# The first chunk's up product as plain 512-column products: a change at the start of a fused attention and mixture-of-experts kernel

## Chip, cores, metric

One core of a Trainium2 chip. The metric is device microseconds of one execution. The kernel before takes 1763.5 us in the runs beside the changed kernel. Repeats of one kernel differ by 1 to 3 us, so differences below about 2 us need several runs and some care.

## The reference

An attention without softmax feeds a mixture of four experts (float32 throughout):

```python
kv  = einsum('bhsd,bhse->bhde', k, v)        # (8, 8, 64, 64); q, k, v: (8, 8, 576, 64)
o   = einsum('bhsd,bhde->bhse', q, kv)
o   = o / sqrt(mean(o*o, -1) + 1e-6) * g_norm
x   = o.transpose(0, 2, 1, 3).reshape(4608, 512)
p   = domain_probs / (domain_probs.sum(-1) + 1e-9)
for e in range(4):                           # w1: (4, 512, 1024), w2: (4, 1024, 512)
    out += p[:, e:e+1] * (relu(x @ w1[e]) @ w2[e])
```

## The kernel before

The 4608 rows of x are cut into nine chunks of 512. A *stage* is one chunk with one expert, and there are 36 of them. Each stage has an **up product** (x by w1), a ReLU and a **down product** (by w2). Attention for the next chunk is mixed into the stages of expert 0.

The up product saves multiplications with Strassen's scheme, used twice: seven times seven products in place of eight times eight. Each of the 49 is done as two matmuls of 128x128x128, 98 in all. For this it needs sums of blocks of w1 and sums of blocks of x, and its results have to be totalled again by VectorE and ScalarE:

```python
for i, m in enumerate(OUTER):                 # 7 outer products
    for j, mm in enumerate(ORDER):            # 7 inner products
        def product(eng, ...):
            for u in range(2):
                nc.tensor.matmul(ps.ap[:, u*P:(u+1)*P],            # 128 columns
                    lhsT=w1f[e][m][mm][1]()[:, u*P:(u+1)*P], rhs=views[m][mm][1](), ...)
        # ... cut: copies out of PSUM (ScalarE), totals (VectorE)
```

Nothing is issued in program order. Each operation is given to a planner with a **key**, its wished place in units of stages. `plan.layout` sorts each engine's work by key, places it by modelled durations, and picks the buffers. An operation may be given to "either" VectorE or GpSimd; that choice, too, is the planner's. While the next operation's key is below 0 and TensorE has nothing to do, the planner puts in **dummies**, two transposes of the identity into an idle bank:

```python
attention(0, -2.0, 1.3, 0.1)                  # chunk 0's attention
weights_1(0, -2.5, 0.02, -0.35)               # loads of w1[0], and sums of its blocks (key -0.35)
x_views = {0: x_forms(0, -0.3)}               # sums of blocks of chunk 0's x
...                                           # cut: for each stage s: attention(c + 1), up, down
order = plan.layout(slots, later, idle, ("u1", "u2", "db"), 0.0)   # dummies' banks; up to key 0
```

PSUM has eight banks in four pairs: u1 and u2 (up), db (down), ab (attention and down).

## Time and profile before

| | before |
|---|---|
| median of the runs beside the changed kernel | 1763.53 us (1762.25 to 1764.72, 4 runs) |
| span of the profiled run | 1762.9 us |
| TensorE lost, 0 to 130 us | 36.0 us |
| TensorE lost after 130 us | some 5 us at the very end, the same after the change |

"Lost" needs a word, since the busy share hides it. The profile counts a dummy as busy, and counts a matmul at half clock as busy too. I therefore count the passes of every shape in a stretch (a float32 product is recorded as two passes; a pass that crosses the end of a stretch is shared out between the two) and multiply by the pace of that shape at full clock (us per pass: 512 columns 0.430, 256 0.2163, 128 0.1117, the attention's 96x64 0.0355, 64x64 0.098). That is the *work*; the stretch less the work, dummies not counted as work, is the *loss*. Four stretches are used: up to 25.6 us (loads pace chunk 0's attention), 25.6 to 62.6, 62.6 to 92, and 92 to 130 us.

### The profile page before, as it was taken

How to read it: one execution, taken by the hardware profiler on the slowest of the kernel's cores; microseconds unless marked ns; L12 is line 12 of the kernel's file. 1: busy time of each engine (PE TensorE's matmuls, PEld its weight loads, DVE VectorE, ACT ScalarE, POOL GpSimd, SP SyncE). 2: the span in 40 equal slices, each digit the busy share in tenths (PEclk: the TensorE clock that was granted, in tenths of full speed). 3: DMA queues.
4: the chain of work that ended last, by engine and by line, in shares of the span. 5: the costliest groups of instructions: out<-in, count | busy, mean ns of one | idle time of the engine just before them, and what ended most of it. 6: DMA issues, size and time to landing. Idle time of an engine off the chain costs nothing.

```text
span 1762.9 us, 36292 instructions
## 1 busy us (share of the span) xinstructions
PE 1748.7 (99%) x14152; PEld 1679.4 (95%) x14152; DVE 1126.9 (64%) x1903; ACT 817.7 (46%) x1913; POOL 850.8 (48%) x822
## 2 busy tenths in 40 slices
PE   9899999999999999999999999999999999999998
PEld 8899999999999999999999999999999999999997
DVE  4764554554665577777674577777674567777654
ACT  3554444444333445555543445555543445555541
POOL 3854544554344534445455635555554634444520
PEclk9999999999999999999999999999999999999999
DMA  9754534541443434444465434444465434444441
GB/s 230 241 172 135 167 101 152 165 145 60 151 137 122 118 95 111 108 109 108 119 161 140 108 96 108 109 109 109 109 173 139 108 97 109 110 109 112 108 113 36
DMA packets 148587, 220.79 MB, mean 125 GB/s; under 512 B 49600, under 2 KB 90816, under 8 KB 148416
## 3 DMA queue, kind: packets, MB, share of 16 engines
q1 hardware_dynamic: 133312, 191.21, 34.7%
q0 software_dynamic: 15104, 27.27, 10.9%
q8 instruction: 111, 1.82, 0.4%
q14 instruction: 60, 0.49, 0.1%
HBM read 145.30 MB, written 73.14 MB: 124 GB/s over the span
## 4 chain that ended last, share of the span: by engine, by line
PE 97%; POOL 1%; DVE 1%; DMA 0%; issue 0%; SPq 0%; ACT 0%; POOLq 0%; DVEq 0%; ACTq 0%
PE u L804 44%; PE db L968 18%; PE db L1041 13%; PE ab L1041 10%; PE ab L968 6%; PE ab L597 1%; PE ab L579 1%; PE u L1166 1%; PE ab L607 1%; PE ab L564 1%; POOL rt L516 1%; PE ab L646 0%; POOL big L339 0%; DMA small<-in_q_dram 0%; POOL xf L339 0%; PE db L597 0%
## 5 line engine op out<-in xcount | busy, mean ns | idle before, releaser
L828 DVE TENSOR_TENSOR big<-u,snap 128x256 f32<-128x256 f32 x717 | 298.8, 422 | 306.8 <-PE u L804 221.4
L804 PE MATMUL u<-xf,big 128*128 128x128 f32 x3312 | 464.0, 275 | 0.1
L820 ACT ACTIVATE snap<-u 128x256 f32<-128x256 f32 x756 | 289.8, 384 | 343.8 <-PE u L804 279.9
L339 DVE TENSOR_TENSOR big<-big,big 128x1024 f32<-128x1024 f32 (+1 forms) x360 | 416.8, 1172 | 28.7 <-ACT big L787 13.6
L804 PEld LDWEIGHTS u<-xf,big 128*128 128x128 f32 x3312 | 426.4, 192 | 7.8 <-ACT snap L820 0.3
L804 PE MATMUL u<-xf,w1y 128*128 128x128 f32 x2700 | 378.7, 276 | 0.0
L804 PEld LDWEIGHTS u<-xf,w1y 128*128 128x128 f32 x2700 | 340.8, 192 | 2.2
L339 POOL TENSOR_TENSOR big<-big,big 128x256 f32<-128x256 f32 (+1 forms) x178 | 249.3, 1405 | 179.6 <-DVE big L339 70.0
L968 PE MATMUL db<-big,big 128*128 128x256 f32 x1336 | 315.8, 380 | 0.0
L968 PEld LDWEIGHTS db<-big,big 128*128 128x128 f32 x1336 | 241.6, 190 | 26.9 <-issue 0.2
L787 ACT ACTIVATE big<-big 128x1024 f32<-128x1024 f32 x131 | 137.7, 1053 | 18.5 <-DVE big L339 12.8
L820 ACT ACTIVATE big<-u 128x256 f32<-128x256 f32 x239 | 91.7, 384 | 106.6 <-PE u L804 101.4
L938 POOL DMA_DIRECT2D out_dram<-big x110 | 100.6, 978 | 72.6 <-ACT big L915 54.0
L1066 ACT ACTIVATE snap<-db 128x256 f32<-128x256 f32 x216 | 76.7, 355 | 111.6 <-PE db L1041 100.7
L339 POOL TENSOR_TENSOR big<-big 128x512 f32<-128x512 f32 (+1 forms) x75 | 89.7, 1201 | 64.2 <-DVE big L339 49.4
L1074 DVE TENSOR_TENSOR big<-ab,snap 128x256 f32<-128x256 f32 (+1 forms) x204 | 78.9, 387 | 63.1 <-PE ab L1041 39.9
L915 ACT ACTIVATE big<-db,p_all 128x256 f32<-128x256 f32 x104 | 49.3, 474 | 140.3 <-PE db L968 140.3
L1102 POOL TENSOR_TENSOR big<-big 128x512 f32<-128x512 f32 x19 | 24.2, 1272 | 163.5 <-DVE big L339 163.5
L922 DVE SCALAR_TENSOR_TENSOR big<-db,p_all,big 128x256 f32<-128x256 f32 x85 | 41.0, 483 | 87.4 <-PE db L968 87.0
L1041 PE MATMUL db<-big,big 128*128 128x128 f32 x688 | 95.6, 275 | 0.0
L1041 PEld LDWEIGHTS db<-big,big 128*128 128x128 f32 x688 | 86.2, 192 | 0.1
L968 PE MATMUL ab<-big,big 128*128 128x256 f32 x344 | 80.5, 379 | 0.0
(191 smaller groups left out, 2517.4 us busy)
## 6 DMA issues: line engine op xcount, KB each, us to landing
xf<-x SPq DMA_DIRECT2D x108, 512.0 KB, 3.5
out_dram<-big POOLq DMA_DIRECT2D x94, 256.0 KB, 5.5
xf<-x_h SPq DMA_DIRECT2D x81, 256.0 KB, 3.0
xf<-x SPq DMA_DIRECT2D x81, 256.0 KB, 3.2
x<-xf SPq DMA_DIRECT2D x36, 512.0 KB, 3.9
big<-in_moe_w_dram SPq DMA_DIRECT2D x28, 512.0 KB, 4.9
small<-in_q_dram SPq DMA_DIRECT2D x72, 128.0 KB, 4.1
kv<-in_k_dram SPq DMA_DIRECT2D x30, 288.0 KB, 3.3
```

Of the source, the lines that this page charges most:

```text
L339: lambda eng: adder(eng).tensor_tensor(out=out_(), in0=a(), in1=b(), op=op),
L787: lambda eng: nc.scalar.activation(out=b.ap[:], in_=b.ap[:], func=ACT.Relu),
L804: nc.tensor.matmul(ps.ap[:, u * P:(u + 1) * P], lhsT=w1f[e][m][mm][1]()[:, u * P:(u + 1) * P], rhs=views[m][mm][1](), start=(mm in (1, 2, ...
L820: lambda eng: nc.scalar.activation(out=where(), in_=ps.ap[:, 0:HN], func=ACT.Copy),
L828: lambda eng: nc.vector.tensor_tensor(out=block(whole, a, t), in0=src.ap[:, 0:HN], in1=add_.ap[:], op=ALU.add),
L915: lambda eng: nc.scalar.activation(out=cell(i, half), in_=ap(), func=ACT.Copy, scale=prob()),
L922: lambda eng: nc.vector.scalar_tensor_tensor(out=cell(i, half), in0=ap(), scalar=prob(), in1=cell(i, half), op0=ALU.mult, op1=ALU.add,),
L938: nc.gpsimd.dma_start(out=dst, in_=cell(i)[parts, :], accum_op=ALU.add)
L968: nc.tensor.matmul(ps.ap[:, 0:HN], lhsT=four(h[m])[:, kt // 2, t, kt % 2, :], rhs=w2f[e][m].ap[:, kt * HN:(kt + 1) * HN], start=(m in (1, ...
L1041: nc.tensor.matmul(ps.ap[:, o * P:(o + 1) * P], lhsT=b.ap[:, col:col + P], rhs=w2q[e][m][mm][1]()[:, kt, :], start=(mm in (1, 2, 5) and o ...
L1066: lambda eng: nc.scalar.activation(out=where(), in_=group_of(ps.ap), func=ACT.Copy),
L1074: lambda eng: nc.vector.tensor_tensor(out=cell(tq, dq), in0=group_of(src.ap), in1=group_of(add_.ap), op=ALU.add,),
```

## The change

The intent: TensorE spends most of its first 6 us after chunk 0's attention on dummies, because the first up product cannot start before all of x and the sums are there. A plain product needs no sums, and its first half needs heads 0 to 3 only.

The diff, cut to its core:

```diff
-        form(need + 0.25, 5, 21, 4, ALU.add)          # sums of w1 blocks
-        ...
+        def sums():
+            form(need + 0.25, 5, 21, 4, ALU.add)
+            ...
+        return sums                                    # called later
...
-            bank = Buf("ab" if b else "u1", f"kv{n}")
+            bank = Buf("ab" if b else "ab", f"kv{n}")
...
-            bank = Buf("ab" if b else "u2", f"xT{n}")
+            bank = Buf("ab" if b else "db", f"xT{n}")
...
+    def up_plain(s, e, c, key, span):
+        ...
+        for i in range(8):                             # 8 units: 128 of the 1024 hidden rows
+            bank = Buf("u1" if a == 0 else "u2", f"up{s}_{i}")
+            for dh in range(2):                        # heads 0-3, then 4-7
+                def product(eng, w=w, bank=bank, dh=dh, ut=2 * a + u):
+                    for kt in range(2):
+                        nc.tensor.matmul(
+                            bank.ap[:], lhsT=two(w.ap[:])[:, kt, ut * P:(ut + 1) * P],
+                            rhs=two(xh[dh].ap[:])[:, kt, :], ...)     # 512 columns
+                plan.add(
+                    key + span * i / 8 - (1.1 if i < 4 and dh == 0 else 0.0), ...)
+            for th, n in ...:                          # two ReLUs by ScalarE for each bank
+        add(0.6, 7, 1, 21, ALU.subtract)               # the down product's sums, 4 in all
...
-    weights_1(0, -2.5, 0.02, -0.35)
-    x_views = {0: x_forms(0, -0.3)}
+    sums_1 = weights_1(0, -2.5, 0.02, 0.3)
+    up_plain(0, 0, 0, 0.0, 1.0)
+    sums_1()
+    x_forms(0, 0.3)
+    x_views = {}
...
-    order = plan.layout(slots, later, idle, ("u1", "u2", "db"), 0.0)
+    order = plan.layout(slots, later, idle, ("ab", "db"), 0.0)
```

So the change has four parts: the plain product; its first halves put ahead (the 1.1); the sums later (keys -0.35 and -0.3 to 0.3); and the banks.

More of the change, by code (lines that the diff above doesn't have):

```diff
@@ L376, in norm_probs @@
         plan.add(key, {"DVE": 1.5}, norm, reads=[probs], writes=[probs])
-    w1f, w2f, w2q = {}, {}, {}
+    w1f, w2f, w2q, w1corner = {}, {}, {}, {}
     ORDER = (1, 2, 6, 5, 7, 4, 3)
@@ L399, in weights_1 @@
         corner = {}
+        w1corner[e] = {}
         for i, (n, dh, uh) in enumerate(((1, 0, 0), (2, 1, 0), (21, 0, 1), (4, 1, 1))):
             corner[n] = Buf(None, f"w1c_{e}_{n}")
+            w1corner[e][uh, dh] = f[n], corner[n]
             load(
@@ L413, in form @@
             )
-        form(need + 0.25, 5, 21, 4, ALU.add)
-        form(need + 0.26, 6, 5, 1, ALU.subtract)
-        form(need + 0.5, 7, 1, 21, ALU.subtract)
-        form(need + 0.5, 3, 2, 6, ALU.subtract)
-        w1f[e] = {}
-        for j, m in enumerate(OUTER):
-            x, low, y = f[m], corner[m], Buf("w1y", f"w1y_{e}_{m}")
-            parts = {}
-            for n, (uq, kt) in ((1, (0, 0)), (2, (0, 1)), (7, (1, 0)), (4, (1, 1))):
-                parts[n] = (
-                    [x, low] if n == 7 else [x],
-                    lambda x=x, uq=uq, kt=kt: two(x.ap[:])[:, kt, uq * HN:(uq + 1) * HN],
-                )
-            for n, at in ((5, 0), (6, 1), (3, 2)):
-                parts[n] = ([y], lambda y=y, at=at: y.ap[:, at * HN:(at + 1) * HN])
-            for o, a, b, op in (
-                (5, 7, 4, ALU.add), (7, 1, 7, ALU.subtract), (6, 5, 1, ALU.subtract),
-                (3, 2, 6, ALU.subtract),
-            ):
-                combine(
-                    need + j / 7, either(HN), parts[o][1], parts[a][1], parts[b][1], op,
-                    parts[a][0] + parts[b][0], [low] if o == 7 else [y],
-                )
-            w1f[e][m] = parts
+        def sums():
+            form(need + 0.25, 5, 21, 4, ALU.add)
+            form(need + 0.26, 6, 5, 1, ALU.subtract)
+            form(need + 0.5, 7, 1, 21, ALU.subtract)
+            form(need + 0.5, 3, 2, 6, ALU.subtract)
+            w1f[e] = {}
+            for j, m in enumerate(OUTER):
+                x, low, y = f[m], corner[m], Buf("w1y", f"w1y_{e}_{m}")
+                parts = {}
+                for n, (uq, kt) in ((1, (0, 0)), (2, (0, 1)), (7, (1, 0)), (4, (1, 1))):
+                    parts[n] = (
+                        [x, low] if n == 7 else [x],
+                        lambda x=x, uq=uq, kt=kt: two(x.ap[:])[:, kt, uq * HN:(uq + 1) * HN],
+                    )
+                for n, at in ((5, 0), (6, 1), (3, 2)):
+                    parts[n] = ([y], lambda y=y, at=at: y.ap[:, at * HN:(at + 1) * HN])
+                for o, a, b, op in (
+                    (5, 7, 4, ALU.add), (7, 1, 7, ALU.subtract), (6, 5, 1, ALU.subtract),
+                    (3, 2, 6, ALU.subtract),
+                ):
+                    combine(
+                        need + j / 7, either(HN), parts[o][1], parts[a][1], parts[b][1], op,
+                        parts[a][0] + parts[b][0], [low] if o == 7 else [y],
+                    )
+                w1f[e][m] = parts
@@ L871, in up, with add @@
         hidden[s] = h
+    def up_plain(s, e, c, key, span):
+        h = hidden[s] = {n: Buf("big", f"h{n}_{s}") for n in (1, 21, 4, 2, 7, 5, 6, 3)}
+        corners = w1corner[e]
+        xh = x_halves(c)
+        for i in range(8):
+            uh, a, u = i // 4, i // 2 % 2, i % 2
+            bank = Buf("u1" if a == 0 else "u2", f"up{s}_{i}")
+            for dh in range(2):
+                w, low = corners[uh, dh]
+                def product(eng, w=w, bank=bank, dh=dh, ut=2 * a + u):
+                    for kt in range(2):
+                        nc.tensor.matmul(
+                            bank.ap[:], lhsT=two(w.ap[:])[:, kt, ut * P:(ut + 1) * P],
+                            rhs=two(xh[dh].ap[:])[:, kt, :], start=(dh == kt == 0),
+                            stop=(dh == kt == 1), skip_group_check=True,
+                        )
+                plan.add(
+                    key + span * i / 8 - (1.1 if i < 4 and dh == 0 else 0.0), pe(2, NT), product,
+                    reads=[w, low, xh[dh]], **({"parts": [bank]} if dh else {"writes": [bank]}),
+                )
+            for th, n in enumerate((1, 21) if uh == 0 else (2, 4)):
+                plan.add(
+                    key + span * i / 8, act(HN),
+                    lambda eng, bank=bank, b=h[n], a=a, u=u, th=th: nc.scalar.activation(
+                        out=four(b)[:, a, :, u, :], in_=two(bank.ap[:, th * HN:(th + 1) * HN]),
+                        func=ACT.Relu,
+                    ),
+                    reads=[bank], parts=[h[n]],
+                )
+        def add(at, to, a, b, op=ALU.add):
+            combine(
+                key + span * at, either(2 * NT), lambda: h[to].ap[:], lambda: h[a].ap[:],
+                lambda: h[b].ap[:], op, [h[a], h[b]], [h[to]],
+            )
+        add(0.6, 7, 1, 21, ALU.subtract)
+        add(1.0, 5, 21, 4)
+        add(1.0, 6, 5, 1, ALU.subtract)
+        add(1.1, 3, 2, 6, ALU.subtract)
     def result(s, e, c, base):
@@ L1148 @@
             if e + 1 < E and c == NCH - 1:
-                weights_1(e + 1, s + 0.0, 0.12, s + 0.3)
+                weights_1(e + 1, s + 0.0, 0.12, s + 0.3)()
                 inner[e + 1] = weights_2(e + 1, s + 1.0, 0.12, s + 2.5)
@@ L1155 @@
                     x_views[s + 1] = x_again((c + 1) % NCH, s + (0.05 if e else 0.6), 0.13)
-            up(s, e, x_views.pop(s))
+            if s:
+                up(s, e, x_views.pop(s))
             if c == 1 and e:
```

## The prediction

> **What bounds the kernel now.** I read the page first (busy shares, the forty slices), then a table of stretches, then the chain of work in order of time, then TensorE's waits.
>
> ```profile
> PE 1748.7 (99%) x14152; PEld 1679.4 (95%) x14152; DVE 1126.9 (64%) x1903; ACT 817.7 (46%) x1913; POOL 850.8 (48%) x822
> PE   9899999999999999999999999999999999999998
> ```
>
> TensorE is busy 99% of the span, but the only slice with a dent near the start is among the first two (44 us each). Part of that "busy" is not work either: L1166 is a dummy transpose of the identity that the kernel issues while it waits at the start. So the span is a sum: TensorE's real work, plus what it loses. The table of stretches (columns: length, busy us and instructions of PE, PEld, DVE, ACT, POOL, then granted clock, DMA share, GB/s) shows where it loses.
>
> ```profile
> 25.60:92.00 66.40, 59.80 (x581) 55.74 (x579) 52.74 (x98) 33.26 (x78) 52.49 (x53) 0.95 0.86 233
> ...
> 62.60:66.50 3.90, 3.88 (x17) 3.33 (x17) 2.86 (x8) 1.07 (x2) 3.73 (x4) 0.50 0.49 189
> 92.00:130.00 38.00, 38.00 (x299) 35.05 (x298) 23.09 (x38) 17.00 (x40) 22.09 (x25) 1.00 0.53 177
> ...
> 430.00:1730.00 1300.00, 1300.00 (x10480) 1267.81 (x10479) 879.26 (x1475) 615.39 (x1453) 622.65 (x590) 1.00 0.44 116
> ```
>
> After 92 us TensorE never waits; before that it does, and for 3.9 us it runs at a clock of 0.50. So an added microsecond of TensorE work after 92 us costs a microsecond, and only losses before 92 us can be won back. The chain in order of time gives both the paces and the first loss:
>
> ```profile
> 24.72 0.89 PE db L597 x8
> 25.61 1.75 PE u L1166 x16
> 27.36 0.44 PE u L607 x4
> 27.80 3.27 PE u L1166 x30
> 31.07 0.44 PE u L607 x4
> 31.51 0.89 PE u L804 x8
> ...
> 120.29 3.46 PE db L968 x16
> ...
> 1651.77 4.02 PE u L804 x36
> ```
>
> From 25.6 to 31.1 us TensorE does only dummies, except for the two transposes of x (L607) for heads 4 to 7, because the first up product needs all four head pairs and sums of them. An fp32 pass of 128 columns takes 4.02/36 = 0.1117 us, one of 256 columns 3.46/16 = 0.2163. An fp32 product is two passes.
>
> ```profile
> PE ab L607 <- DVE small L523: 3.4, 3, 2.1
> PE ab L597 <- ACT big L613: 0.8, 1, 0.8
> PE ab L579 <- ACT small L569: 0.7, 1, 0.7
> ...
> 38.69 0.61 ACT small L502
> 39.32 0.70 DVE ss L507
> 40.09 0.31 POOL ss L512
> 40.48 1.90 POOL rt L516
> ```
>
> TensorE's open waits (total, times, longest) are for chunk 1's attention: its normalization runs ScalarE, VectorE, GpSimd, VectorE (the last four lines, from the chain), and VectorE and GpSimd are at the same time full of sums of weights and of x.
>
> **The loss from 25.6 to 92 us.** Passes in that stretch, by line, times their pace: up products 228 x 0.1117 = 25.5; attention products 49 x 0.1117 = 5.5 and 16 x 0.1117 = 1.8; transposes 58 x 0.11 = 6.4 and 16 small ones x 0.098 = 1.6; key-value products 144 x 0.0355 = 5.1; down products 8 x 0.2163 = 1.7. Sum 47.5 us of work in 66.4 us: 18.9 us are lost. The parts: dummies 62 passes, 6.8 us; open waits 6.4 us (those with a releaser); the half clock about 2 us (it halves 3.9 us); the rest, some 3.7 us, are gaps of 0.1 us or so at changes of instruction.
>
> **What the Trainium skill says.** (1) "TensorE: Matmul & The Clock Gate", Part 1, says that an idle window of about 3.4 us halves the PE clock until it has been busy again. The trace agrees: 2.1 us of waiting and three shorter waits around 56 to 62 us come just before the 0.50 stretch. (2) The same page, section "Wait — 56ns, not 53.3ns?", gives back-to-back spacings of 55.6 ns at 128 columns and 215.7 ns at 512. Here an fp32 pass of 128 takes 111.7 ns, twice that; doubling the page's 215.7 estimates a 512 pass at 0.431 us. No 512-column product is in this trace. (3) "PSUM — Partial Sum Buffer", rule 1, allows at most 512 columns, one bank, per product: the plain product uses a bank whole, so the four u banks allow four units in flight. (4) "GPSIMD Engine Reference", section 1, says that GpSimd shares its SBUF interfaces with VectorE instructions of two SBUF inputs. The trace agrees that something like it costs: a VectorE sum of 128x256 at 29.86 us took 1.48 us beside a GpSimd sum, others 0.42.
>
> **The change part by part.**
> *Removed:* 98 up products of 128 columns in chunk 0 (7 x 7 x 2, confirmed by the counts of the two programs: 3528 against 3430), 98 x 2 x 0.1117 = 21.9 us. Also 21 VectorE totals from PSUM, 28 ScalarE copies, and most of the combining adds of 128x1024 for chunk 0.
> *Added:* 32 products of 512 columns. The two measured paces give 0.1046 us per 128 columns, so a pass of 512 is 0.2163 + 2 x 0.1046 = 0.4255 (0.431 from the page). 64 passes: 27.2 to 27.6 us. Net: +5.3 to +5.7, say 5.5 us of work on the bounding engine, because the plain form does no saving of multiplications.
> *Moved earlier:* in the changed order, right after the last attend of chunk 0 (ends 25.6 us), come four half units over heads 0 to 3, 4 x 2 x 0.851 = 6.8 us, with the two transposes between them. Their x half is ready (ScalarE wrote it at 24.8 us) and 5.7 MB had landed by 25 us, enough for the 3.4 MB of q, k, v and the four weight blocks of 0.5 MB. They fill the place of the dummies. The last transpose slips from 31 to about 33 us behind them; its x half is then ready at about 34.3, and only 8 dummy passes (0.9 us) are left in the order there.
> *Moved later:* the sums of weights and of chunk 0's x are no longer before the first product; chunk 0 needs no sums of either. They have until chunk 1's up. From 34.6 us TensorE has 12 half units with kt pairs (12 x 1.70 = 20.4 us) plus chunk 1's attention and the start of chunk 2's (about 10 us) without any sum: to about 65 us. I followed each attention chain by hand through the changed orders: VectorE, GpSimd and VectorE return in 4.5 to 7 us, and TensorE has 1.5 to 3 us more than that in hand. After 70 us, where the sums of chunk 1's second x half, a GpSimd form of w2 (2.3 us) and the remainder's normalization meet, I find one wait of about 1.5 us and some small ones.
> *Banks:* key-value results go to the two ab banks, transposed x to db. The extra waits I see in the order fall on dummies.
>
> **Sum.** Loss 25.6 to about 90 us after the change: 0.9 dummies, about 3 of waits, about 2 of small gaps, no half clock: 5.9. So 1763 - 18.9 + 5.9 + 5.5 = 1755.5 us. I round to 1755: 8 us, 0.5%.
>
> **Rivals.**
> *The sums only move.* VectorE and GpSimd together do the same sums; if they pile up at 65 to 95 us, the 6.4 us of waits and the half clock return there, and the net is -5.9 (dummies) + 5.5 (work): about 1763. For it: 52.7 and 52.5 of 66.4 us busy in the stretch. Against: chunk 0 no longer asks for its 21 totals (about 7 us) and some six adds (1.1 us each on VectorE, 2.3 on GpSimd), so there is less to do, and it may be spread over 30 us in which TensorE needs no sums.
> *All of it works and nothing waits.* Losses fall to the 0.9 and small gaps: about 1751.
> *The plain product costs more than its pace,* from banks drained late (two ScalarE halves per bank) or weight blocks that land late: each wait of 1 us adds 1 us; with 5 us the gain is nearly gone, 1760.
> *Another end.* The planner lays out the whole program anew; slots differ everywhere. A stall in the steady part could cost some us, but before it had 0.1 us of waiting from 92 to 1730 us, so I give it little.
>
> **Range and chances.** The ends of the range are the second rival's 1751 less a us, and the third's 1760 with a us. The ceiling of any gain is all 18.9 us lost, 1.1% of the span, so faster by 2% (35 us) isn't to be had; slower by 2% would need 35 us of new stalls in a part that has none. 0.01 each.
>
> **What would show it right or wrong.** Right: products of 512 columns from 25.6 us on, 0.85 us each, about 27.4 us in all; no L1166 counterpart beyond some 10 passes after 25.6 us; granted clock 1.00 from 40 to 80 us; open waits of TensorE after 25 us of about 3 us; the steady part as before. Wrong: a stretch between 65 and 95 us with TensorE open and waits for VectorE or GpSimd sums (first rival); waits of the 512-column products for ScalarE or a DMA (third); any idle after 130 us (fourth).

## More of the kernel before

The prediction shows the main lines. One more view of before is needed later, three stretches around its half clock. Columns are length; busy us and instructions of PE, PEld, DVE, ACT, POOL; granted clock; DMA share; GB/s.

```profile
59.00:60.60 1.60, 1.16 (x8) 0.97 (x8) 1.60 (x4) 0.35 (x2) 1.52 (x2) 1.00 0.84 186
60.60:67.50 6.90, 4.88 (x21) 4.33 (x22) 4.80 (x11) 2.17 (x4) 6.69 (x8) 0.52 0.54 178
67.50:70.00 2.50, 2.50 (x23) 2.50 (x23) 2.25 (x6) 1.16 (x3) 1.33 (x4) 0.96 0.64 184
```

The third number from the end of each line is the clock: for 6.9 us it is about half. Only 21 passes get done there, in 4.88 us of busy time, against 23 in the following 2.5 us.

## The result

| | before | after |
|---|---|---|
| median, us | 1763.53 (1762.25 to 1764.72) | 1754.54 (1754.10 to 1755.88) |
| ratio | | 0.995 (95%: 0.9933 to 0.9968) |
| profiled span, us | 1762.9 | 1752.3 |
| lost 0 to 25.6 us | 15.9 | 14.3 |
| lost 25.6 to 62.6 us (dummies in it) | 14.5 (6.8) | 1.8 (0.9) |
| lost 62.6 to 92 us | 4.4 | 2.9 |
| lost 92 to 130 us | 1.1 | 1.2 |

A ratio here is the mean time of one kernel's runs over that of the other's of the same rounds, so not quite the ratio of the medians quoted. The gain is 9.0 us in the medians.

The page of the changed kernel:

```profile
span 1752.3 us, 35867 instructions
...
PE 1744.0 (100%) x13970; PEld 1659.0 (95%) x13970; DVE 1119.1 (64%) x1904; ACT 808.8 (46%) x1897; POOL 826.0 (47%) x793
...
PE   9999999999999999999999999999999999999998
```

The second digit of the PE row was 8 and is 9: the dent near the start is gone. The same stretches as before:

```profile
25.60:92.00 66.40, 64.91 (x459) 45.71 (x458) 50.40 (x101) 28.01 (x70) 37.75 (x35) 1.00 0.89 251
...
62.60:66.50 3.90, 3.90 (x43) 2.71 (x41) 3.44 (x7) 1.91 (x6) 2.45 (x3) 1.00 0.89 263
...
92.00:130.00 38.00, 38.00 (x323) 34.80 (x322) 18.47 (x34) 18.74 (x44) 17.50 (x17) 1.00 0.48 140
```

Three things stand in the first line. The clock is 1.00 (before 0.95). TensorE is open for 1.5 us (66.40 less 64.91; before 6.6). And GpSimd is busy for 37.75 us instead of 52.49. That isn't the doing of the sums' new place: in e8, with the sums early, it is 36.49. The plain form itself leaves less to add. The middle line stood at a clock of 0.50 before. The chain in order of time shows what took the dummies' place (start, length, what, passes):

```profile
23.26 0.89 PE db L602 x8
24.15 1.72 PE u L891 x4
25.87 0.44 PE db L612 x4
26.31 5.15 PE u L891 x12
31.46 0.44 PE db L612 x4
31.90 0.44 PE ab L569 x4
32.33 0.87 PE ab L1219 x8
```

L891 is the plain product, L1219 the dummies, L612 the transposes of x, L602 the attend, L569 the transposes of q. Right after the last attend come 16 passes of the plain product, with x's two transposes between them; 8 dummy passes are left. The 12 passes in 5.15 us give the pace: 0.430 us for one of 512 columns.

TensorE's waits (total, times, longest), the first and third of which lie in the start:

```profile
PE ab L1219 <- POOL ident masks.py:199: 1.3, 1, 1.3
PE ab L569 <- ACT big L618: 0.8, 1, 0.8
PE ab L569 <- DMA small<-in_q_dram: 0.5, 1, 0.5
PE ab L651 <- ACT big L618: 0.4, 1, 0.4
PE ab L666 <- DVE small L528: 0.3, 1, 0.3
```

The waits for the normalization (L523 before, L528 now) went from 3.4 to 0.3 us. The chain shows that it is still a tight one:

```profile
69.08 0.70 DVE ss L512
...
70.14 1.64 POOL rt L521
71.77 0.00 issue
71.77 1.27 POOL xf L339
...
74.01 1.90 POOL rt L521
...
75.94 0.69 DVE small L528
...
76.68 0.46 PE ab L666 x4
```

The second power (L521, of the rows left over from the chunk) has to get behind a sum on GpSimd (L339), yet TensorE waits just 0.3 us for its result.

**The account.** The whole difference lies before 130 us, and it adds up. With the work that the plain form adds, 64 x 0.430 less 196 x 0.1117, which is 5.6 us, the loss falls from 36.0 to 20.3 us: 1762.9 - 15.7 + 5.6 = 1752.8, and the profiled span is 1752.3.

This profile was of the fastest run, and its start lost 1.6 us less than that of before. A second set of runs (below, e0) gives a start of 15.9 us, as before's, and so shows that as chance; there the account is 36.0 - 21.9 = 14.1 us won, 5.6 paid: 8.5 us, for 9.0 in the profiled spans.

### The profile page after: what moved, and what is told of

It reads as the page before. It is cut to its first block, busy times and chain, and to the rows that moved or that the text cites. A ratio compares the mean times of both kernels' runs of the same rounds, so it can differ in the third digit from the quotient of the medians. Undisturbed runs are those within 1.5% of the kernel's fastest.

```text
span 1752.3 us, 35867 instructions
## 1 busy us (share of the span) xinstructions
PE 1744.0 (100%) x13970; PEld 1659.0 (95%) x13970; DVE 1119.1 (64%) x1904; ACT 808.8 (46%) x1897; POOL 826.0 (47%) x793
## 4 chain that ended last, share of the span: by engine, by line
PE 98%; SPq 1%; DMA 0%; POOL 0%; DVE 0%; issue 0%; ACT 0%
PE u L809 44%; PE db L1017 19%; PE db L1090 13%; PE ab L1090 10%; PE ab L1017 6%; PE u L891 2%; PE ab L602 1%; PE ab L584 1%; PE ab L612 1%; PE ab L569 1%; SPq L345 1%; DMA big<-in_v_dram 0%; PE ab L651 0%; POOL rt L521 0%; PE ab L666 0%; PE ab L636 0%
## 5 line engine op out<-in xcount | busy, mean ns | idle before, releaser
L833 DVE TENSOR_TENSOR big<-u,snap 128x256 f32<-128x256 f32 x696 | 290.6, 422 | 304.1 <-PE u L809 217.9
L809 PE MATMUL u<-xf,big 128*128 128x128 f32 x3248 | 453.9, 275 | 0.0
L825 ACT ACTIVATE snap<-u 128x256 f32<-128x256 f32 x735 | 281.7, 384 | 339.0 <-PE u L809 276.8
L339 DVE TENSOR_TENSOR big<-big,big 128x1024 f32<-128x1024 f32 (+1 forms) x354 | 410.6, 1175 | 32.9 <-ACT big L792 13.1
L809 PEld LDWEIGHTS u<-xf,big 128*128 128x128 f32 x3248 | 417.4, 192 | 7.3 <-issue 0.2
L809 PE MATMUL u<-xf,w1y 128*128 128x128 f32 x2652 | 371.6, 275 | 0.0
L809 PEld LDWEIGHTS u<-xf,w1y 128*128 128x128 f32 x2652 | 334.3, 192 | 2.0
L339 POOL TENSOR_TENSOR big<-big,big 128x256 f32<-128x256 f32 (+1 forms) x177 | 247.0, 1399 | 179.6 <-DVE big L339 67.2
L792 ACT ACTIVATE big<-big 128x1024 f32<-128x1024 f32 x127 | 133.5, 1052 | 17.9 <-DVE big L339 12.4
L339 POOL TENSOR_TENSOR big<-big 128x512 f32<-128x512 f32 (+1 forms) x75 | 89.6, 1200 | 63.0 <-DVE big L339 36.6
```

The lines of the kernel that those rows point to most:

```text
L339: lambda eng: adder(eng).tensor_tensor(out=out_(), in0=a(), in1=b(), op=op),
L792: lambda eng: nc.scalar.activation(out=b.ap[:], in_=b.ap[:], func=ACT.Relu),
L809: nc.tensor.matmul(ps.ap[:, u * P:(u + 1) * P], lhsT=w1f[e][m][mm][1]()[:, u * P:(u + 1) * P], rhs=views[m][mm][1](), start=(mm in (1, 2, ...
L825: lambda eng: nc.scalar.activation(out=where(), in_=ps.ap[:, 0:HN], func=ACT.Copy),
L833: lambda eng: nc.vector.tensor_tensor(out=block(whole, a, t), in0=src.ap[:, 0:HN], in1=add_.ap[:], op=ALU.add),
```

## The experiments

The text below says "the theory" for the sum in the prediction. All twelve were run in five rounds; they gave four to six timings each, beside runs of before on the same chip (medians 1763.51 for e1 to e4, 1763.9 for e0 and e5 to e7, 1764.05 for e8 to e11). All results are correct but e4's.

### e1: without the early halves

```diff
-                    key + span * i / 8 - (1.1 if i < 4 and dh == 0 else 0.0), pe(2, NT), product,
+                    key + span * i / 8, pe(2, NT), product,
```

> The changed kernel with one term taken out: the plain half units over heads 0 to 3 are no longer put ahead (no -1.1 in their key), so every plain product comes after all of x. Theory (the early half units fill TensorE's wait for heads 4 to 7): dummies come back between 24 and 31 us, x is complete about 2 us sooner because its last transpose no longer queues behind 6.9 us of products, so 6.9 - 2.3 = 4.6 us slower than the changed kernel, 5 us before-minus-this instead of 9 (about 1759). Rival (the gain is all from moving the sums away): within 1 us of the changed kernel, 1754.5.

Measured: 1759.84 us, ratio 0.9976 (0.9963 to 0.9988), 5.3 us above the changed kernel. The profile has 3.7 us of dummies after 25.6 us against 0.9, a wait of 1.3 and one of 0.8 us for the normalization, and a stretch from 77 to 84 us with a clock of 0.76. The early halves are worth what the theory said, though only 2.8 us of it are dummies and the rest is waits and clock.

### e2: the sums back where they were

```diff
-    sums_1 = weights_1(0, -2.5, 0.02, 0.3)
+    sums_1 = weights_1(0, -2.5, 0.02, -0.35)
-    x_forms(0, 0.3)
+    x_forms(0, -0.3)
```

> The changed kernel with the other term taken out: plain product and early halves stay, but the sums of weights and of chunk 0's x get back the early keys of the kernel before (need -0.35, x forms -0.3), so VectorE and GpSimd do them between 27 and 45 us, at the same time as chunk 1's attention. Theory (the plain product gives 30 us without need of sums, so VectorE and GpSimd have slack wherever the sums stand): waits of TensorE between 34 and 65 us grow to 0 to 2 us, the end 0 to 2 us later than the changed kernel, 1754.5 to 1756.5. Rival (moving the sums later is what took the waits away): the 6.4 us of waits and the half clock are back, 6 to 8 us slower, about 1761 to 1763.

Measured: 1758.43 us, ratio 0.997 (0.9957 to 0.9982), 3.9 us above the changed kernel, which neither the theory (up to 2) nor the rival (6 to 8) had. The waits for the normalization are back:

```profile
PE ab L612 <- DVE small L528: 2.6, 2, 1.9
```

and the chain names what holds them up:

```profile
70.29 2.35 POOL big L339
...
72.72 0.21 POOL ss L517
...
73.00 2.79 POOL rt L521
...
75.82 0.70 DVE small L528
...
76.56 0.67 PE ab L612 x4
```

A sum of 128x1024 on GpSimd (2.35 us) stands ahead of the normalization's power, which itself takes 2.79 us; the one at 70.14 us of the changed kernel, of the same 128x8 elements, took 1.64. The profiled run was the fastest, 1757.04 us at a mean clock of 1.000; the two slowest, 1759.31 and 1760.25 us, had 0.998. So part of the 3.9 us is a half clock that comes in some runs only.

### e3: only the banks

```diff
-            bank = Buf("ab" if b else "u1", f"kv{n}")
+            bank = Buf("ab" if b else "ab", f"kv{n}")
-            bank = Buf("ab" if b else "u2", f"xT{n}")
+            bank = Buf("ab" if b else "db", f"xT{n}")
-    order = plan.layout(slots, later, idle, ("u1", "u2", "db"), 0.0)
+    order = plan.layout(slots, later, idle, ("ab", "db"), 0.0)
```

(on the kernel before)

> The kernel before with only the bank part of the change: chunk 0's key-value results in ab, its transposed x in db, dummies in ab and db. Theory (banks only make room for the plain units): same as before within 1.5 us, 1763. Rival (the banks freed u1 and u2 for chunk 0's first products and so part of the gain): 2 us or more faster.

Measured: 1765.85 us, ratio 1.0013 (1.0000 to 1.0027). That is 2.3 us above before, a little outside the 1.5 that the theory allowed, and on the slow side. The banks alone give nothing. By the program they free the u banks for the early halves; early halves without them were not run.

### e4: the plain form once more, in the steady part

```diff
+            if s == 3:
+                x_views.pop(s)
+                up_plain(s, e, c, s + 0.0, 1.0)
-            if s:
+            elif s:
                 up(s, e, x_views.pop(s))
```

(and the early key for stage 0 alone; the corner of w1 that no longer exists by then is replaced by another, so the result is wrong, by 0.175 relative)

> The changed kernel with a second plain up product, for chunk 3 (about 130 us in, where TensorE has no wait), and a wrong result there on purpose (the block of w1 that the sums have dropped is replaced by another of its size). It measures the price of the plain form where nothing is there to fill. By the 0.430 us that a pass of 512 columns took in the changed kernel's trace: 64 x 0.430 - 196 x 0.1117 = 27.5 - 21.9 = 5.6 us slower than the changed kernel, 1760. By the extrapolated pace of 0.4255: 5.3 us. Rival (the plain form is cheaper than that in the steady part because it frees VectorE and ScalarE of totals and copies): less than 3 us.

Measured: 1760.16 us, ratio 0.998 (0.9967 to 0.9992): 5.6 us above the changed kernel, 5.7 above the runs of e0. Where TensorE never waits, a plain stage costs just its work, 5.6 us. This is the price that the gain at the start pays.

### e0: the changed kernel again

No edit; it serves as the neighbour of e5 to e7.

> The changed kernel unaltered, as the common measure for the three runs beside it. Its first profile began the attention 1 to 1.5 us sooner than the profile of before, with the same loads issued in the same order at the same times; if that is chance, its second profile need not show it, and the median is again 8 to 10 us below before: 1754 to 1755.

Measured: 1754.45 us, ratio 0.9946 (0.9932 to 0.9959), profiled span 1753.9 us; the start loses 15.9 us, and the rest 6.0, as in the first profile.

### e5: the early halves head pair by head pair

```diff
-            for dh in range(2):
+            for hp in range(4):                       # one matmul for each pair of heads
+                dh, kt = divmod(hp, 2)
...
-                    key + span * i / 8 - (1.1 if i < 4 and dh == 0 else 0.0), pe(2, NT), product,
-                    reads=[w, low, xh[dh]], ...
+                    key + span * i / 8 if i > 3 else key - 1.1 + 0.1 * hp + 0.02 * i,
+                    pe(1, NT), product, reads=[w, low], holds=[xh[dh]], after=[xw[c, hp], *done], ...
```

> The changed kernel with the early part cut finer: each of the first four plain units goes head pair by head pair (one product of 128 rows at a time as soon as that quarter of x is there), so heads 4 and 5 are no longer held back until both halves are ready and the last transpose queues behind single products. Theory (what the change recovers before 35 us is limited by the grain at which x becomes usable): the 0.9 us of dummies at 32 us and some 0.7 us before 24 us go, 1.5 us faster than the changed kernel, 1753. Rival (the loads pace that part, the grain is nothing): within 0.5 us of it.

Measured: 1755.86 us, ratio 0.9954 (0.9941 to 0.9968). A miss: 1.4 us slower where 1.5 faster was expected. The last dummies did go, but in the new plan chunk 1's attention waits instead (L613 and L585 are the transposes of x and the key-value product here):

```profile
61.55 0.65 PE L613 MATMUL ab<-ident,small 128*128 128x128 f32 x4 [0.84 <-DVE small L529]
...
62.98 0.92 PE L585 MATMUL ab<-kv,kv 96*64 96x64 f32 x24 [0.78 <-ACT big L619]
```

### e6: e5, and the loads of w1 earlier

```diff
-    sums_1 = weights_1(0, -2.5, 0.02, 0.3)
+    sums_1 = weights_1(0, -2.85, 0.2, 0.3)
```

> e5 with the first 0.5 MB block of w1 loaded before q, k, v of heads 4 to 7, the second after them. Theory (before 24 us the plain units wait for the weight block, since their first quarter of x is ready at about 19 us; 0.5 MB take 2.2 us at the 235 GB/s of that stretch, so the later heads come 2.2 us later but the plain units over heads 0 to 3, 6.9 us, start about 3 us sooner): 1 to 3 us faster than e5, 1750 to 1752. Rival (what is loaded first only shifts who waits): the same as e5 within 1 us, or slower.

Measured: 1756.34 us, ratio 0.9956 (0.9943 to 0.9968). A miss too: the stretch to 62.6 us loses just 1.2 us, but 62.6 to 92 us loses 4.5.

### e7: no dummies at all

```diff
-    order = plan.layout(slots, later, idle, ("ab", "db"), 0.0)
+    order = plan.layout(slots, later, idle, ("ab", "db"), -9.0)
```

> The changed kernel without any dummy transposes. Theory (the dummies hold the granted clock at 1.00, as the half clock after the waits at 56 to 62 us in the kernel before suggests): clock 0.50 for the first 24 us and for some us of the first plain units, which then take up to twice as long; 2 to 5 us slower than the changed kernel, 1756.5 to 1759.5. Rival (the loads pace the start, so the clock is nothing there): within 1 us.

Measured: 1753.4 us (1752.89 to 1756.43), ratio 0.9943 (0.993 to 0.9955), against 0.9946 for e0 beside it. A miss: 2 to 5 us slower was expected, and it is the same. The first passes do run at half pace:

```profile
12.17 1.92 PE L602 MATMUL db<-kvbd,small 128*128 128x128 f32 x8
...
16.04 1.12 PE L602 MATMUL db<-kvbd,small 128*128 128x128 f32 x8
```

The same eight passes take 1.92 us at 12 us and 1.12 at 16. But that lies beside the loads: at the start TensorE waits 10.5 us for DMAs (6.8, 2.3 and 1.4 us in three lines of waits), so a slower pass only shortens the next wait. The start loses 15.7 us, and 15.9 in e0. The granted clock in the table of stretches doesn't show it:

```profile
10.00:15.00 5.00, 4.61 (x48) 4.22 (x46) 0.24 (x1) 1.63 (x4) 0.00 (x0) 1.00 1.18 224
```

The table prints 1.00 where the trace has no clock record: in this trace the first one begins at 15.18 us, between the two groups of passes shown, while in the other profiles, all with dummies, it begins at 4 to 10 us. So the dummies had kept the passes fast at a time when they do not set the end.

### e8: the plain product by itself

Both edits of e1 and e2.

> Both terms taken out at once: the plain product stands where the old up product stood, no half unit ahead, sums and x forms with their early keys. So far: the early halves were worth 5.3 us (e1 against the changed kernel), the later sums 4.0 (e2). Theory (the two are separate, the one fills dummies, the other spares VectorE and GpSimd): they add, 1754.5 + 9.3 = 1763.8, no gain left over before. Rival (each does the other's work in its absence, because the sums fit beside dummies): 1759 to 1761.

Measured: 1758.36 us, ratio 0.9972 (0.9957 to 0.9986). Had the parts simply added up, it would have stood at 1763.8; the rival's 1759 to 1761 is nearer, though the result lies just below it. The profile shows dummies both before and between the transposes (column: start, length, what):

```profile
24.18 1.91 PE L1219 MATMUL ab<-ident 128*128 128x128 f32 x16
25.93 0.60 PE L612 MATMUL db<-ident,small 128*128 128x128 f32 x4
26.37 3.44 PE L1219 MATMUL ab<-ident 128*128 128x128 f32 x30
29.64 0.60 PE L612 MATMUL db<-ident,small 128*128 128x128 f32 x4
30.08 1.88 PE L891 MATMUL u<-big,big 128*128 128x512 f32 x4
```

The start loses as much as before's, and the same 46 dummy passes stand there. But after them come products that need no sums of blocks, and the loss from 25.6 to 92 us falls from 19.0 to 7.4 us all the same. That is 11.6 us won for 5.6 paid. The stretch as a line (columns as before):

```profile
25.60:92.00 66.40, 65.12 (x459) 44.99 (x458) 51.77 (x98) 26.40 (x66) 36.49 (x35) 1.00 0.81 227
```

GpSimd (36.49 us) has 16 us less to do in this stretch than before, although the sums stand early; VectorE is as busy as before (51.77 us, before 52.74). Two things thus came together with the plain form: TensorE's products need no sums, and there are fewer totals, copies and combining adds to do. No run parts them. The early halves (e2, 1758.43) or the late sums (e1, 1759.84) added to it give nothing by themselves; both together give the other 4 us.

### e9: early sums again, the wide ones kept off GpSimd

The edit of e2, and

```diff
-                k_, either(1024), ...
+                k_, (either if e else dve)(1024), ...            # sums of w1 and w2 of expert 0
-                key + span * at, either(2 * NT), ...
+                key + span * at, dve(2 * NT), ...                # the four sums of chunk 0's result
```

> e2 (sums early) with every sum of 128x1024 of the first chunk (forms of w1 and w2 of expert 0, combining adds of the plain product) on VectorE alone. In e2's trace the two long waits of TensorE (1.9 and 0.7 us) come behind a GpSimd power that took 2.8 us in place of 1.64, one of them after a 2.35 us GpSimd sum. Theory (e2 lost its 4 us to wide GpSimd sums in and beside the normalization): waits fall from 3.9 to 2 us or less, 2 us faster than e2, 1756.5. Rival (VectorE is the one that is short of time; the same sums there delay it more): e2 or slower, 1758.5 to 1761.

Measured: 1755.78 us, ratio 0.9954 (0.994 to 0.9968), 2.7 us below e2, as expected. The waits for the normalization fall from 2.6 to 1.5 us:

```profile
PE ab L612 <- DVE small L528: 1.5, 2, 1.0
```

All five runs have clocks of 0.999 or 1.000. So most of what e2 lost (2.7 of 3.9 us) goes with the wide sums on GpSimd, not with the early place alone. What e9 took away is the sum ahead of the power: the power itself still took 2.61 us (at 71.46 us of its trace). How much of the 2.7 us is the new layout is not shown; e10 is a warning.

### e10: the same rule on the changed kernel

> The changed kernel with the same rule (128x1024 sums of the first chunk on VectorE alone). Theory: 1.5 us of waits are left there, of which 0.3 is behind the normalization; 0 to 1 us faster, 1753.5 to 1754.5. Rival as in e9: 1 us or more slower.

Measured: 1757.36 us, ratio 0.9963 (0.995 to 0.9976). A miss: up to 1 us faster was expected, and it is about 3 slower. Its five runs are in two groups: 1755.30, 1755.73 and 1757.36 us at a clock of 1.000, 1758.38 and 1759.98 at 0.998. The profile is of the last:

```profile
70.80:77.70 6.90, 4.97 (x29) 3.95 (x28) 4.36 (x8) 2.87 (x6) 6.49 (x7) 1.00 0.52 152
77.70:84.60 6.90, 6.88 (x47) 5.91 (x48) 6.23 (x17) 2.60 (x7) 2.49 (x5) 0.52 0.47 174
```

A stretch in which TensorE is open for 1.93 us in all (the longest wait 1.4 us, for the normalization) is followed by 6.9 us at half clock, in which it is busy all the time. Here the clock costs some 3 us (half of 6.9), and in other runs of the same program nothing.

### e11: the sums later still

```diff
-    sums_1 = weights_1(0, -2.5, 0.02, 0.3)
+    sums_1 = weights_1(0, -2.5, 0.02, 0.6)
-    x_forms(0, 0.3)
+    x_forms(0, 0.6)
```

> The changed kernel with the sums put off further (need and x forms 0.6 in place of 0.3). Theory (what counts is that they keep out of the way of chunk 1's attention, and 0.3 does that already while chunk 1's up needs them at 1.0): 0 to 2 us slower, 1754.5 to 1756.5, with waits for sums at 65 to 75 us. Rival (later is better all the way from -0.35): 1 us or more faster.

Measured: 1757.42 us, ratio 0.9964 (0.9951 to 0.9977), 2.9 us above the changed kernel, a little more than expected. The profiled start lost 16.7 us, so a part of it is chance; 62.6 to 92 us lost 4.3.

### All together

Losses are us of the profiled run. "Account" is 1762.9 plus the loss from 0 to 130 us less 36.0, plus 5.6 for each plain stage. The table is my own count of passes, not a view of the profile.

| run | median | lost to 25.6 | to 62.6 (dummies) | to 92 | to 130 | account | span |
|---|---|---|---|---|---|---|---|
| before | 1763.53 | 15.9 | 14.5 (6.8) | 4.4 | 1.1 | | 1762.9 |
| after | 1754.54 | 14.3 | 1.8 (0.9) | 2.9 | 1.2 | 1752.8 | 1752.3 |
| e0 | 1754.45 | 15.9 | 1.9 (0.9) | 2.9 | 1.2 | 1754.4 | 1753.9 |
| e1 no early halves | 1759.84 | 15.9 | 4.6 (3.7) | 4.8 | 0.9 | 1758.7 | 1758.4 |
| e2 early sums | 1758.43 | 14.7 | 2.6 (0.9) | 4.8 | 1.2 | 1755.8 | 1755.3 |
| e3 banks | 1765.85 | 15.9 | 14.1 (4.8) | 5.2 | 1.4 | 1763.6 | 1763.2 |
| e4 plain twice | 1760.16 | 14.9 | 1.8 (0.9) | 2.9 | 1.2 | 1759.0 | 1758.4 |
| e5 by pair | 1755.86 | 14.6 | 2.6 (0) | 3.5 | 1.2 | 1754.3 | 1753.9 |
| e6 w1 first | 1756.34 | 15.5 | 1.2 (0) | 4.5 | 1.2 | 1754.9 | 1754.6 |
| e7 no dummies | 1753.4 | 15.7 | 1.0 (0) | 3.5 | 1.1 | 1753.8 | 1753.6 |
| e8 plain alone | 1758.36 | 15.9 | 5.6 (3.7) | 1.8 | 1.3 | 1757.1 | 1756.8 |
| e9 early, wide on VectorE | 1755.78 | 15.1 | 2.4 (0.9) | 2.9 | 1.3 | 1754.2 | 1754.1 |
| e10 wide on VectorE | 1757.36 | 15.9 | 1.8 (0.9) | 7.2 | 1.2 | 1758.6 | 1758.2 |
| e11 sums later | 1757.42 | 16.7 | 1.8 (0.9) | 4.3 | 1.2 | 1756.4 | 1756.1 |

The account meets the span within 0.6 us every time. So the steady part did not change in any of these kernels, though the planner laid each out anew, and the four stretches hold all that there is to explain. None of the edits beats the changed kernel by more than its scatter; e7 is its equal.

## Why the prediction was right

It said 1755 us, 1750 to 1761; the result is 1754.5. Step by step:

- **The work added, 5.5 us:** 5.6 us by the measured pace. The pace of a 512-column pass doubled from the Trainium skill's "TensorE: Matmul & The Clock Gate", section "Wait — 56ns, not 53.3ns?" (estimate 0.431) was the better of the two estimates, the one drawn out from 128 and 256 columns (0.4255) a little low. e4 measured the price by itself.
- **The loss before, 18.9 us:** 19.0 by the count of the table.
- **The loss after, 5.9 us:** 4.8 us in both profiles, the first and e0's. The term for dummies (0.9) is exact. That for waits (3) was too large: after 25 us the three waits listed are 1.5 us together. That for gaps (2) is then 2.4 us (4.8 - 0.9 - 1.5). The wait of about 1.5 us that I had traced by hand near 75 us is one of 0.3.
- **No half clock:** so it is; every run of the changed kernel and of e0 has a mean clock of 0.999 or 1.000, every run of before beside e0 to e11 0.997 or 0.998. Its length before was misread, though: I took the stretch that I had cut, 3.9 us, for the whole; it lasts 6.8 us, from 60.9 to 67.7 in the trace's clock records. The sum did not suffer, since the loss was counted from passes and not from its parts.
- **Start and steady part the same:** so they are, within 0.1 us in e0. The first profile's faster start is chance.
- **The rivals:** that the sums would pile up later is false for this change, as waits for sums didn't come back; but e2 and e10 show that it was near. Late banks: TensorE's waits have no line of L891, so false. A new stall in the steady part: false.

The onset of that half clock was misread too. A sentence that is cut from the prediction had the wait of 2.1 us come before it, in agreement with the page. That wait began at 60.5 us (59.32 + 1.16) and lay almost wholly inside the half clock:

```profile
59.32 1.16 PE L597 MATMUL ab<-kvbd,small 128*128 128x128 f32 x8 [0.47 <-ACT small L639]
62.62 1.11 PE L607 MATMUL ab<-ident,small 128*128 128x128 f32 x4 [2.14 <-DVE small L523]
```

In the 6.8 us before its onset stand only three waits of 0.5 to 0.7 us and 0.4 us of the long one. What starts a half clock is not shown here.

What the prediction had **not right is where the gain comes from**. It let the early halves take the place of all the dummies (5.9 us), and the late sums do the rest. e8 shows that the plain product alone, with early sums and without early halves, already wins about half (0.28% of before's time in e8, 0.54% in e0), dummies falling from 6.8 to 3.7 us and the other losses from 12.2 to 3.7. What ends may be TensorE's dependence on sums while attention's normalization needs the same two engines, or the load on these engines itself; that is argued, not shown. The other two parts act only together. So the total came out right for a sum whose parts had been given to the wrong causes.

Open: how much of the 1 to 3 us in e5, e6, e10 and e11 is the edit and how much is the new layout that any edit brings, including the half clock that some runs of some layouts have. Two runs of the same edit with different layouts would tell; none was made. Open too: which of the plain form's two effects, products without sums or less work for GpSimd and ScalarE, gives its half.

## What to carry to other kernels

Where one engine is saturated for nearly the whole span, write the time as that engine's work plus its losses, and count the losses from passes and paces instead of busy time, which hides dummies and a slow clock. A costlier form without preparation (5.6 us more work here) paid here at the start, where the bound engine had waits and dummies (some 15 us of loss gone), and not in the steady part, where the same form costs all of its 5.6 us. Parts of such a change don't add up, so test each alone and in pairs before saying which one gave the gain, and don't trust 2 us when the edit re-plans everything.

## What the Trainium skill lacked or had wrong

- "TensorE: Matmul & The Clock Gate" gives no spacing for fp32 (other pages tell of its passes and its peak rate, not of a measured spacing). Here an fp32 product is recorded as two passes of 0.1117 us at 128, 0.2163 at 256 and 0.430 us at 512 columns, each about twice the page's spacing for its width.
- The same page makes an idle window of some 3.4 us the cause of the half clock, and advises "No PE-idle gaps >~3µs"; of shorter idles it tells for another kernel, without a size. Here shorter waits came before it: 1.93 us open within 6.9, the longest wait 1.4 us, then 6.9 us at 0.52 (e10); in the kernel before, three waits of 0.5 to 0.7 us and 0.4 us of a fourth, then 6.8 us. Other runs of e10's program had no half clock (mean clock 1.000 against 0.998; 1755.3 against 1760.0 us).
